# A table of offsets for the steps of a list-scheduled attention and MLP kernel

## The chip, the cores and the metric

The kernel runs on one core of a Trainium2 chip. The core has TensorE (matrix products), VectorE, ScalarE and GpSimd (element-wise work), and SyncE, whose instruction stream here issues nearly all DMAs. Each engine runs its own instructions in the order in which they were written; between engines there are only semaphores. The metric is the time of one execution on the device, in microseconds (us).

## The reference

Attention over 4 batches, 12 heads, 448 positions and head size 64, then two gated MLPs in a row on what it gives. Cut to its core:

```python
q_n = q / sqrt(mean(q*q) + 1e-6) * g_q           # k likewise
scores = q_n @ k_n.T / sqrt(64)
attn = exp(scores - max(scores)); attn = attn / (sum(attn) + 1e-9)
x = attn @ v                                     # to (4, 448, 768)

h = maximum(x @ w_in, 0)                         # MLP 1: 768 -> 1024
conv = sum(conv_w[k] * hp[:, k:k+S] for k in range(3))
x = (h * sigmoid(conv)) @ w_out                  # 1024 -> 768

gate_pre = sum(conv_w2[k] * xp[:, k:k+S] for k in range(5))   # MLP 2, causal
out = (sigmoid(gate_pre) * (x @ w_val)) @ w_out2 # 768 -> 768 -> 768
```

## The kernel before

All values are float32 outside. Inside, a product is made of three float16 products (high by high, low by high, high by low), so most tiles exist as a high half and a low half. The low half is the value minus the high half.

Attention is cut into 84 units u, 21 for each batch, each with 128 rows of scores for two heads (the remainder rows of several heads are put together in "rem" units). The steps of a unit are functions: `qk` (score matmuls into a pair of PSUM banks; ps<-ka,qa), `smax` (row maximum on VectorE; ps<-ps, then mx<-ps,root), `sexp` (two exponentials on ScalarE, which free the banks; p<-ps,mx,root), `phi` and `plo` (high and low half of p; p<-p and p<-p,p), `ptr` (a DMA transpose issued by SyncE; pt<-p) and `av` (product with v; ps<-vm,pt and ps<-vv,pt). Of two tiles each, the even units use p_0 and pt_92, the odd ones p_1 and pt_93; mx has four buffers in turn. Three units finished on a pair of heads give a tile of x: `x_pair` scales it (ps<-ps,rs), makes the high half (x<-ps), the low half (x<-ps,x), which frees the bank, and has both transposed by DMA (act<-x). `prep` loads q and k, sums their squares (ssq), takes the row factors (half, root) and transposes them (qa<-tq, ka<-tk); `load_v` and `split_v` prepare v (vst, vv, vm).

In batch 0, which has no MLP work beside it yet, p and x are transposed on TensorE instead.

The MLPs of a batch follow in tiles: `w_in_tile` (8 tiles f of 128 channels; ps<-act,wi), convolution, gate and high and low half, `w_out_tile` (ps<-act,wo), `w_val_tile` (ps<-act,wv), and `out_tile` (ps<-w,act, four blocks c of rows: three of 128 in two halves of 384 columns, and the remaining 64 rows in both halves at once), whose `evac` copies to osb on ScalarE and stores (out_dram<-osb). MLP work of one batch is placed between the attention units of the next.

What sets the order: a step is not run where the code is written but placed at a time with `at(t, fn)`. The steps are sorted by that time, and `run` records their operations in a `Plan`. `order` then makes a list schedule: every operation gets a due value, `first`, from the time of its step and the length of the work behind it (its tail); each engine in turn takes the ready operation with the smallest value, and an operation that several engines could do goes to another engine if that one would be done sooner. A few passes are made in which `first` is mixed with times found backward from the end, and the best by the planner's own length is kept. `emit` writes the instructions in that order, all from one line (378 in the profile of before, 495 after), so the rows are told apart by their tiles. The due value before:

```python
first = [o[4] * (1.0 - self.URGENT) - tail[i] * self.URGENT for i, o in enumerate(ops)]
```

Of the kernel before, what the change touches and what calls it, by code (L numbers as in the profile page):

```python
# [9 lines left out]
F32 = mybir.dt.float32  # L10
# [4 lines left out]
AF = mybir.ActivationFunctionType  # L15
# [7 lines left out]
SW = 2.0 ** UPW  # L23


class Plan:


# [6 lines left out]

    ENGINES = ("tensor", "vector", "scalar", "gpsimd", "sync")
    HOP = {"tensor": 0.2, "vector": 0.13, "scalar": 0.16, "gpsimd": 0.09}
    WINDOW = 20.453
    AHEAD = 42.251
    URGENT = 0.596  # L40
    TICK = 10.24 / 3
# [23 lines left out]
    def __init__(self):  # L65
        self.ops = []
        self.live = {}
        self.now = self.floor = 0.0
        self.tensor, self.vector, self.scalar, self.gpsimd, self.sync = (
            Plan.Queue(self, e) for e in Plan.ENGINES  # L70
        )
# [48 lines left out]
    def run(self, t, fn, *a):  # L120

        self.now = t
        fn(*a)

    def depend(self, engine, reads, out):
# [38 lines left out]
    def add(self, ways, **lean):  # L164
        engine, _, a, k = ways[0]
        aps = [x for x in list(a) + list(k.values()) if isinstance(x, bass.AP)]
        out = k.get("out", aps[0])
        flow, after = self.depend(engine, [x for x in aps if x is not out], out)
        costs = {}
        for e, m, a, k in ways:  # L170
            aps = [x for x in list(a) + list(k.values()) if isinstance(x, bass.AP)]
            costs[e] = (self.cost(e, m, a, k, aps, k.get("out", aps[0])), m, a, k)
        window = self.AHEAD if ways[0][1] == "dma_start" and k["in_"].dtype in (I64, U32) else self.WINDOW
        release = max(self.now - window, self.floor) if ways[0][1] == "dma_start" else 0.0
        self.ops.append((costs, flow | after, release, lean, self.now))

    def cost(self, engine, method, a, k, aps, out):

# [62 lines left out]
    def order(self):  # L241
        ops, nops = self.ops, len(self.ops)
        users = [[] for _ in ops]
        for i, o in enumerate(ops):
            for d in o[1]:
                users[d].append(i)
        tail = [0.0] * nops
        port, shape = [], []
        for i in range(nops):
            port.append({})  # L250
            shape.append(None)
            for e, (_, method, a, k) in ops[i][0].items():
                aps = [x for x in list(a) + list(k.values()) if isinstance(x, bass.AP)]
                port[i][e] = self.shares(e, method, aps, k.get("out", aps[0]))
                if e == "tensor":
                    shape[i] = (a[1].shape[0] <= 64, a[0].shape[0] <= 64)
        for i in reversed(range(nops)):
            (busy, lag, data), method, *_ = next(iter(ops[i][0].values()))
            tail[i] = max((tail[u] for u in users[i]), default=0.0) + busy + (data + 2.0 if method.startswith("dma") else 0.15)
        first = [o[4] * (1.0 - self.URGENT) - tail[i] * self.URGENT for i, o in enumerate(ops)]  # L260
        best = None
        for _ in range(self.PASSES):
            result, length, ends = self.forward(first, users, port, shape)
            if best is None or length < best[1]:
                best = result, length
            late = self.backward(result, length, ends, users)
            first = [self.MIX * a + (1.0 - self.MIX) * b for a, b in zip(first, late)]
        result, self.length = best
        self.times = {i: t for t, _, i, _ in result}
        self.engine = {i: e for _, _, i, e in result}  # L270
        return [(i, e) for _, _, i, e in result]
# [110 lines left out]
def kernel(  # L382
# [71 lines left out]
    cw2 = sb.tile([P, NC2 * KD], F32, tag="cw2", name="cw2")  # L454
    ident = sb.tile([P, P], F32, tag="ident", name="ident")
    zero = sb.tile([P, 1], F32, tag="zero", name="zero")

    banks = pp.tile([P, 8, 512], F32, tag="ps", name="ps")

# [14 lines left out]

        nc.vector.scalar_tensor_tensor(out, x, c, y, ALU.mult, op1)

    def copy(lean, out, x):

        nc.add([("vector", "tensor_copy", (out, x), {}), ("scalar", "activation", (out, x, AF.Copy), {})], vector=lean)

    def times(lean, out, x, c):

# [17 lines left out]
    S_DQ = 0.156  # L500
    S_K0 = 1.401
    S_K1 = 10.211
    S_DK = 1.263
    S_LQ = 4.632
    S_LK = -0.828
    S_G = -2.951
    DT0 = 2.39
    DT_1 = 5.037
# [2 lines left out]
    LAG = 2  # L511
    A_EXP = 0.154
    C_GATE = 2.001
    C_MUL = 2.338
    C_HI = 2.578
    C_LO = 3.244
    V_HI = 0.203
# [3 lines left out]
    E_PTR = 0.777  # L521
    E_AV = 2.342
    X_LAG = 2.135
    MPE = 97.144
    M_0 = 2.618
    M_1 = -6.504
    M_2 = -5.351
# [3 lines left out]
    L_TAP = -0.285  # L531
    LATE = 1
    LATE_F = 11
    FOLD_Q = 0
    FOLD_K = 0
    SIGN_IN = 0
    SIGN_OUT = 0
    SIGN_VAL = 3
# [9 lines left out]
    QD_ = 1.286  # L548
    W_IN = -79.489
    W_IN_STEP = 0.794  # L550
    W_OUT = -19.05
    W_OUT_STEP = 1.022
    W_VAL = 20.994
    W_VAL_STEP = 0.65
# [8 lines left out]
    OUT_1 = 0  # L563
    OUT_2 = 4
    OUT_3 = 4
    FLAT_0 = 0.908
    FLAT_1 = 0.0
    FLAT_2 = 0.0
    WIDE_0 = 1
    WIDE_1 = 1  # L570
    WIDE_2 = 1


    L_SQ = 3.972
# [22 lines left out]
    ROOTP_2 = 1  # L597
    ROOTP_3 = 0
    L_XLO = 0.9
    L_STEP = -0.143  # L600
    L_PLO = 0.668
    L_VM = -0.571
    L_VHI = 1.418
# [6 lines left out]


    WIDE = [(0, r) for r, w in enumerate((WIDE_0, WIDE_1, WIDE_2)) if w]

    LEAVE_IN = (LEAVE_0, LEAVE_1, LEAVE_2, LEAVE_3)
    X_SBUF = (0, XSB_1, XSB_2, XSB_3)
    ROOT_POOL = (ROOTP_0, ROOTP_1, ROOTP_2, ROOTP_3)
    FLAT = [(0, r) for r, f in enumerate((FLAT_0, FLAT_1, FLAT_2)) if f]
    events = []

    def at(t, fn, *a):  # L620
# [99 lines left out]
    def consts():  # L720

        nc.gpsimd.memset(mx[3], 0.0)
        nc.scalar.activation(mx[3], mx[3], AF.Exp)
        for t in ssq:
            nc.gpsimd.memset(t, 1.0)
        nc.gpsimd.memset(zero, 0.0)

    def init_v(ones, mid):

# [45 lines left out]
    def weight_piece(name, t, dram, dst, post, own, sign):  # L775
        st = {}
        wide = dram.dtype == I64
        n, m = dst[0].shape[1:] if len(dst[0].shape) == 3 else (1, dst[0].shape[1])
        m *= n

        def fetch():
            if not own:
                raw, w = stage(2 * m, st), stage(m, st) if len(dst) == 2 else None
            else:
                area = st["area"] = areas.pop(0)
                raw, w = area[:, 0 : 2 * m], area[:, 2 * m : 3 * m]
            if len(dst) == 1:
                w = dst[0].rearrange("p a b -> p (a b)") if n > 1 else dst[0]
            st["w"] = w
            to, src = (raw.bitcast(U32), dram.bitcast(U32)) if wide else (w, dram)  # L790
            st["raw"] = to
            loaded.append(t)
            load(to.rearrange("p (a b) -> p a b", a=n) if n > 1 else to, src, early=len(loaded) <= EARLY_W)

        def split():
            w = st["w"]
            if wide:
                to_f32(w, st["raw"], UPW, True, sign)
            else:
                nc.gpsimd.tensor_scalar(w, w, SW, None, ALU.mult)  # L800
            if len(dst) == 2:
                if n > 1:
                    w = w.rearrange("p (a b) -> p a b", a=n)
                copy(L_WHI, dst[0], w)
                sub(L_WLO, dst[1], w, dst[0])
            there[name] = there.get(name, 0) + 1
            if own:
                areas.append(st["area"])
            else:
                for x in st["i"]:  # L810
                    give(x)

        at(t, fetch)
        at(post, split)
# [41 lines left out]
    def prep(b, r, t0, tq, dq, tk_, dk, ahead):  # L856
# [23 lines left out]
        def total(fold, out, x):  # L880
            for i in range(0 if solo else fold):
                d = D >> i + 1
                nc.gpsimd.tensor_tensor(x[:, :, 0:d], x[:, :, 0:d], x[:, :, d : 2 * d], ALU.add)
                x = x[:, :, 0:d]
            nc.vector.tensor_reduce(out, x, AX.X, ALU.add)
# [15 lines left out]
        def sum_q():  # L901
            s2 = early_sq if b == 0 else oq.rearrange("p a n -> p (a n)").bitcast(F32)
            s2 = s2.rearrange("p (n d) -> p n d", d=D)
            square(s2, xq)
            total(FOLD_Q, ss[:, 0:NQ], s2)

        def split_q():
            if flat:
                return
            x = xq.rearrange("p n d -> p (n d)")  # L910
            copy(lean(L_QHI, S_LQ), oq[:, 0], x)
            sub(lean(L_QLO, S_LQ), oq[:, 1], x, oq[:, 0])

        def turn_q():
# [24 lines left out]
        def sum_k(i):  # L939
            j, x, x3, o, hi, lo = of_k(i)  # L940
            assert holds["kin", i] == (b, j)
            assert b == 0 or ("tk", 0) not in holds
            s2 = early_sq[:KR] if b == 0 else o.rearrange("p a c d -> p (a c d)").bitcast(F32)
            s2 = s2[:, 0 : 2 * KC * D].rearrange("p (n d) -> p n d", d=D)
            square(s2, x3)
            total(FOLD_K, ss[:KR, cols(i)], s2)

        def gain_k(i):
            x3 = of_k(i)[2]
# [156 lines left out]
    def phi(u):  # L1106
        u.o = p16[u.n % u.bufs]
        if u.out:
            copy(L_PHI, u.o[:, 0], u.p)
        else:  # L1110
            times(L_PHI, u.o[:, 0], u.p, SP)

# [559 lines left out]
```

## Time and profile before

| | us |
|---|---|
| median of 3 runs | 644.56 |
| lowest and highest run | 640.95, 646.72 |
| the profiled execution | 643.0 |
| its span in the trace | 641.2 |
| TensorE busy | 591.9 (92%) |
| VectorE busy | 510.4 (80%) |
| ScalarE busy | 419.6 (65%) |
| GpSimd busy | 254.5 (40%) |

The span is the time from the first to the last record of the trace; the profiled execution's own time holds 1.8 us more around it. An engine is busy while one of its instructions runs. DVE is VectorE, ACT ScalarE, POOL GpSimd, SP SyncE, PE TensorE; a row's start is counted from the start of the span, and the brackets behind it give the idle time of the engine just before and what ended it.

### The profile page before, as it was taken

The page shows a single profiled execution, that of the slowest core. Times are in us where ns is not written, and L with a number is a line of the kernel's source. Part 1 is how long each engine was busy: PE and PEld are TensorE (multiplying, and loading weights), DVE is VectorE, ACT ScalarE, POOL GpSimd, SP SyncE. Part 2 cuts the span into 40 slices and gives each one's busy share as a digit, 9 for nine tenths or more (in the row PEclk, how much of TensorE's full clock was granted, in tenths as well). Part 3 has the DMA queues.
Part 4 walks back from the last instruction along what each step waited for, and adds up shares of the span by engine and source line. Part 5 has one row for each costly group of instructions (what it writes and reads, how often), then busy time and mean ns, then how long its engine had stood idle before and what let it go on. Part 6 is the DMA issues. An engine that isn't in the chain of part 4 may idle for free.

```text
span 641.2 us, 12698 instructions
## 1 busy us (share of the span) xinstructions
PE 591.9 (92%) x4755; PEld 334.8 (52%) x4755; DVE 510.4 (80%) x1011; ACT 419.6 (65%) x739; POOL 254.5 (40%) x308
## 2 busy tenths in 40 slices
PE   4888998997997896999989999989999999999997
PEld 2665676453443443555545556545454565555554
DVE  6988899899999997999768984779898754478620
ACT  4986999798878975897655764768756454262211
POOL 2534675454454654657433552344534011040000
PEclk9985999897997998999989999999999999999999
DMA  8968576995799899867887668794545757100002
GB/s 206 224 162 208 110 184 172 210 220 122 151 194 194 198 199 191 207 143 130 189 155 127 117 127 176 147 170 74 105 80 104 118 119 148 25 0 2 1 13 74
DMA packets 254610, 88.05 MB, mean 137 GB/s; under 512 B 240671, under 2 KB 250453, under 8 KB 254549
## 3 DMA queue, kind: packets, MB, share of 16 engines
q1 hardware_dynamic: 252581, 86.76, 65.1%
q8 instruction: 37, 0.61, 0.4%
q10 hardware_dynamic: 1968, 0.49, 0.4%
q14 instruction: 24, 0.20, 0.1%
HBM read 38.59 MB, written 5.51 MB: 69 GB/s over the span
## 4 chain that ended last, share of the span: by engine, by line
PE 57%; DVE 24%; DMA 8%; ACT 5%; issue 3%; SPq 2%; ACTq 0%; DVEq 0%
PE ps L378 57%; DVE ps L378 6%; DVE act L378 6%; DVE w L378 4%; DVE scr L378 3%; DVE p L378 2%; DMA w<-in_moe_w_val_dram 2%; SPq L378 2%; DMA act<-in_moe_w_out_dram 2%; DMA pt<-p 2%; DVE ssq L378 1%; ACT p L378 1%; DMA w<-in_moe_w_in_dram 1%; ACT act L378 1%; ACT w L378 1%
## 5 line engine op out<-in xcount | busy, mean ns | idle before, releaser
L378 PE MATMUL ps<-act,wi 128*128 128x448 f16 x576 | 121.9, 362 | 7.4 <-DVE act L378 3.4
L378 PE MATMUL ps<-act,wo 128*128 128x448 f16 x576 | 123.6, 361 | 1.3 <-DVE act L378 0.8
L378 DVE TENSOR_REDUCE ps<-ps 128x2 f32<-128x896 f32 x84 | 91.5, 1093 | 21.4 <-PE ps L378 21.2
L378 ACT ACTIVATE p<-ps,mx,root 128x448 f32<-128x448 f32 x112 | 75.2, 721 | 36.1 <-DVE mx L378 20.9
L378 PE MATMUL ps<-w,act 128*128 128x384 f16 (+1 forms) x576 | 92.1, 327 | 1.1 <-DVE act L378 0.8
L378 PE MATMUL ps<-ka,qa 64*128 64x448 f16 (+3 forms) x560 | 81.3, 391 | 11.8 <-DVE p L378 9.3
L378 PE MATMUL ps<-act,wv 128*128 128x448 f16 x432 | 89.8, 353 | 1.5 <-ACT wv L378 1.1
L378 PE MATMUL ps<-vv,pt 128*128 128x65 f16 (+3 forms) x1488 | 88.2, 204 | 0.0
L378 PEld LDWEIGHTS <-wi 128*128 128x128 f16 x576 | 55.3, 100 | 61.7 <-issue 18.7
L378 POOL TENSOR_TENSOR p<-p,p 128x896 f16<-128x896 f32 x28 | 53.0, 1895 | 77.4 <-ACT p L378 50.7
L378 PEld LDWEIGHTS <-wo 128*128 128x128 f16 x576 | 55.2, 100 | 54.4 <-issue 12.1
L378 PEld LDWEIGHTS <-pt 128*128 128x128 f16 (+1 forms) x1512 | 63.6, 101 | 26.5 <-issue 8.3
L378 ACT ACTIVATE act<-ps 128x448 f16<-128x448 f32 (+4 forms) x81 | 43.0, 536 | 49.2 <-PE ps L378 25.6
L378 PEld LDWEIGHTS <-act 128*128 128x128 f16 (+1 forms) x576 | 48.7, 101 | 35.8 <-issue 8.8
L378 DVE SCALAR_TENSOR_TENSOR act<-ps,cw,act 128x446 f32<-128x446 f32 (+3 forms) x96 | 63.6, 676 | 0.9
L378 PEld LDWEIGHTS <-wv 128*128 128x128 f16 x432 | 40.1, 98 | 42.1 <-issue 5.2
L378 DVE SCALAR_TENSOR_TENSOR w<-w 128x768 uint32<-128x768 uint32 (+1 forms) x56 | 45.5, 815 | 0.0
L378 PEld LDWEIGHTS <-qa 64*128 64x128 f16 (+1 forms) x528 | 22.6, 99 | 43.8 <-issue 34.5
L378 DVE SCALAR_TENSOR_TENSOR scr<-ps,cw,scr 128x447 f32<-128x447 f32 x64 | 42.2, 676 | 1.9 <-ACT scr L378 1.6
L378 ACT ACTIVATE p<-p 128x896 f16<-128x896 f32 x42 | 39.8, 949 | 0.4
L378 POOL TENSOR_TENSOR kin<-kin,gb 112x512 f32<-112x512 f32 x22 | 29.2, 1332 | 19.6 <-ACT tk L378 14.6
L378 PE MATMUL ps<-vm,pt 128*128 128x130 f16 (+3 forms) x248 | 29.3, 234 | 5.0 <-DMA pt<-p 3.5
(128 smaller groups left out, 930.9 us busy)
## 6 DMA issues: line engine op xcount, KB each, us to landing
w<-in_moe_w_in_dram SPq DMA_DIRECT2D x8, 768.0 KB, 5.8
w<-in_moe_w_out_dram SPq DMA_DIRECT2D x8, 768.0 KB, 5.2
kin<-in_k_dram SPq DMA_DIRECT2D x24, 224.0 KB, 3.6
act<-in_moe_w_out_dram SPq DMA_DIRECT2D x12, 384.0 KB, 3.7
w<-in_moe_w_val_dram SPq DMA_DIRECT2D x12, 384.0 KB, 4.0
out_dram<-osb SPq DMA_DIRECT2D x24, 192.0 KB, 2.3
qin<-in_q_dram SPq DMA_DIRECT2D x34, 128.0 KB, 3.6
vst<-in_v_dram SPq DMA_DIRECT2D x17, 224.0 KB, 3.5
```

The costliest lines, as they stand in the source:

```text
L378: getattr(getattr(nc, e), method)(*a, **k)
```

## The change

Every step that `run` records now has a number, its place in the sorted list of 2034 steps. A table `OFFSETS` gives about half of these numbers an offset, from −7.05 to 10.73 us, most under 1 us; it is added to the due value of each operation of the step. Besides:

- Constants of the planner are set anew: WINDOW from 20.453 to 22.193 (how long before its step's time a load may be issued), and C_MUL, MPE, W_OUT, S_DK, S_LQ, S_LK, L_STEP by small amounts.
- `copy` may take GpSimd for the high halves of weights, q and p (a multiplication by ones), at a cost of 3.0 us added in the planner's choice.
- The sum of squares of q in batch 3 is folded on GpSimd in halves; the switches for this are now one for each batch.
- A tile of ones is set at the start.

```diff
+OFFSETS = {
+    4: 0.31, 6: 0.41, 7: 0.25, 8: 0.74, 19: -0.21, 20: 6.17, 21: 1.58, 24: -1.85, 27: 0.23, 28: 0.27, 45: 1.9, 46:
...
-    WINDOW = 20.453
+    WINDOW = 22.193
...
     def run(self, t, fn, *a):
 
         self.now = t
+        self.event += 1
         fn(*a)
...
-        self.ops.append((costs, flow | after, release, lean, self.now))
+        self.ops.append((costs, flow | after, release, lean, self.now, OFFSETS.get(self.event, 0.0)))
...
-        first = [o[4] * (1.0 - self.URGENT) - tail[i] * self.URGENT for i, o in enumerate(ops)]
+        first = [o[4] * (1.0 - self.URGENT) - tail[i] * self.URGENT + o[5] for i, o in enumerate(ops)]
...
+    def copy(lean, out, x, pool=None):
+
+        ways = [("vector", "tensor_copy", (out, x), {}), ("scalar", "activation", (out, x, AF.Copy), {})]
+        if pool is None:
+            nc.add(ways, vector=lean)
+            return
+        by = one[: x.shape[0], 0:1].to_broadcast(list(x.shape)) if len(x.shape) == 2 else one[: x.shape[0], 0:1].unsqueeze(2).to_broadcast(list(x.shape))
+        ways.append(("gpsimd", "tensor_tensor", (out, x, by, ALU.mult), {}))
+        nc.add(ways, vector=lean, gpsimd=pool)
...
-            total(FOLD_Q, ss[:, 0:NQ], s2)
+            total(FQ[b], ss[:, 0:NQ], s2)
...
-            copy(lean(L_QHI, S_LQ), oq[:, 0], x)
+            copy(lean(L_QHI, S_LQ), oq[:, 0], x, PC_Q)
...
-            copy(L_PHI, u.o[:, 0], u.p)
+            copy(L_PHI, u.o[:, 0], u.p, PC_P)
```

In the rows of the order below, mx_101 belongs to unit 49 and mx_102 to unit 50, and the number of a tile tells its buffers apart.

SyncE, the transposes of units 49 (pt_93) and 50 (pt_92) and what stands around them, before:

```order
L378 DMA_TRANSPOSE pt_93<-p_1_91 128x14x128
L378 DMA_TRANSPOSE qa_68<-tq_87 128x14x128
L378 DMA out_dram<-osb_99 128x384
L378 DMA qin_85<-in_q_dram 128x4x64 x3
L378 DMA_TRANSPOSE act<-x_0_80 128x3x128 x2
L378 DMA out_dram<-osb_98 64x384 x2
L378 DMA_TRANSPOSE pt_92<-p_0_90 128x14x128
```

and the same place in the changed kernel:

```order
L495 DMA_TRANSPOSE qa_68<-tq_87 128x14x128
L495 DMA_TRANSPOSE pt_93<-p_1_91 128x14x128
L495 DMA out_dram<-osb_99 128x384
L495 DMA qin_85<-in_q_dram 128x4x64
L495 DMA_TRANSPOSE pt_92<-p_0_90 128x14x128
L495 DMA_TRANSPOSE act<-x_0_80 128x3x128 x2
L495 DMA out_dram<-osb_98 64x384 x2
```

Unit 50's transpose has moved ahead of two q loads, two transposes of x and two stores; the q transpose now comes ahead of unit 49's.

VectorE, the row maxima and low halves of the same units, before:

```order
L378 TENSOR_REDUCE ps<-ps 128x2
L378 TENSOR_TENSOR mx_101<-ps,root_106 128x2
L378 TENSOR_SCALAR mx_101<-mx_101 128x2
L378 TENSOR_TENSOR p_1_91<-p_1_89,p_1_91 128x896
L378 TENSOR_REDUCE ssq_104<-tk_86 112x8 x2
L378 TENSOR_SCALAR ssq_104<-ssq_104 128x30
L378 TENSOR_SCALAR half_108<-ssq_104 128x30
L378 TENSOR_SCALAR root_107<-half_108 128x30
L378 TENSOR_TENSOR half_108<-root_107 128x30
L378 TENSOR_REDUCE ps<-ps 128x2
L378 TENSOR_TENSOR mx_102<-ps,root_106 128x2
```

and in the changed kernel:

```order
L495 TENSOR_REDUCE ps<-ps 128x2 x2
L495 TENSOR_TENSOR mx_101<-ps,root_106 128x2
L495 TENSOR_TENSOR mx_102<-ps,root_106 128x2
L495 TENSOR_SCALAR mx_101<-mx_101 128x2
L495 TENSOR_SCALAR mx_102<-mx_102 128x2
L495 TENSOR_TENSOR p_1_91<-p_1_89,p_1_91 128x896
L495 TENSOR_REDUCE ssq_104<-tk_86 112x8 x2
L495 TENSOR_SCALAR ssq_104<-ssq_104 128x30
L495 TENSOR_TENSOR p_0_90<-p_0_88,p_0_90 128x896
```

Both maxima are taken in a row, ahead of the low half of unit 49 and of the row factors (ssq, half, root).

VectorE, about 415 to 423 us of the trace of before: the scaling of an x tile (rs, ps<-ps,rs), unit 64's low half (p_0_90), and the x halves, before:

```order
L378 TENSOR_SCALAR rs_109<-ps 128x6
L378 SCALAR_TENSOR_TENSOR half_108<-root_106 128x30
L378 RECIPROCAL rs_109<-rs_109 128x6
L378 TENSOR_TENSOR p_0_90<-p_0_88,p_0_90 128x896
L378 TENSOR_TENSOR ps<-ps,rs_109 128x6x64
L378 TENSOR_REDUCE ps<-ps 128x2
L378 TENSOR_TENSOR x_0_80<-ps,x_0_80 128x384
```

and in the changed kernel:

```order
L495 TENSOR_SCALAR rs_109<-ps 128x6
L495 RECIPROCAL rs_109<-rs_109 128x6
L495 TENSOR_TENSOR ps<-ps,rs_109 128x6x64
L495 CAST x_0_80<-ps 128x384
L495 TENSOR_TENSOR x_0_80<-ps,x_0_80 128x384
L495 TENSOR_REDUCE ps<-ps 128x2
```

The copy of the high half has come from ScalarE to VectorE (CAST), and the low half p_0_90 no longer stands between the reciprocal and the scaling.

## Rows read from the trace of the kernel before

**Rows 1.** The page: busy time by engine; the group of w_in matmuls.
```profile
PE 591.9 (92%) x4755; PEld 334.8 (52%) x4755; DVE 510.4 (80%) x1011; ACT 419.6 (65%) x739; POOL 254.5 (40%) x308
...
L378 PE MATMUL ps<-act,wi 128*128 128x448 f16 x576 | 121.9, 362 | 7.4 <-DVE act L378 3.4
```

**Rows 2.** Windows by stage: length, busy time (instructions) of PE, PEld, DVE, ACT, POOL, clock, DMA, GB/s.
```profile
0.00:260.00 260.00, 221.49 (x1741) 133.71 (x1742) 235.81 (x479) 209.01 (x374) 131.67 (x189) 0.91 0.84 183
260.00:303.00 43.00, 41.74 (x345) 22.27 (x344) 41.94 (x82) 36.14 (x70) 27.43 (x34) 1.00 0.76 164
303.00:425.00 122.00, 117.44 (x1041) 64.24 (x1040) 90.79 (x188) 72.48 (x119) 50.86 (x47) 0.99 0.76 149
425.00:478.00 53.00, 52.33 (x437) 27.81 (x436) 48.82 (x99) 38.16 (x67) 24.03 (x24) 1.00 0.57 102
478.00:637.00 159.00, 158.93 (x1199) 86.76 (x1197) 93.09 (x167) 63.28 (x110) 20.49 (x18) 1.00 0.30 59
```

**Rows 3.** Timeline of PE, the rows with a wait after 260 us.
```profile
294.19 0.48 PE L378 MATMUL ps<-w,act 128*128 128x384 f16 x2 [0.80 <-DVE act L378]
...
301.30 0.48 PE L378 MATMUL ps<-w,act 128*128 128x384 f16 x2 [0.32 <-POOL w L378]
...
329.94 0.35 PE L378 MATMUL ps<-vm,pt 128*128 128x130 f16 x3 [1.90 <-DMA pt<-p]
...
419.38 0.34 PE L378 MATMUL ps<-vm,pt 128*128 128x130 f16 x3 [0.99 <-DMA pt<-p]
...
422.89 0.54 PE L378 MATMUL ps<-act,wi 128*128 128x448 f16 x2 [1.67 <-DVE x L378]
...
477.58 0.35 PE L378 MATMUL ps<-vm,pt 128*128 128x130 f16 x3 [0.63 <-DMA pt<-p]
```

**Rows 4.** Windows: two half-clocked stretches, and one with waits at full clock.
```profile
44.20:64.60 20.40, 17.32 (x78) 12.58 (x79) 15.94 (x42) 13.57 (x26) 8.77 (x7) 0.50 0.91 205
330.90:334.20 3.30, 3.30 (x11) 1.30 (x9) 1.63 (x3) 1.66 (x3) 0.16 (x1) 0.50 1.08 213
...
419.30:424.00 4.70, 2.95 (x32) 1.81 (x33) 1.68 (x6) 2.55 (x5) 0.93 (x2) 1.00 0.86 167
```

**Rows 5.** Groups of p on DVE: ns of one (least, median, most), first and last start.
```profile
L378 DVE TENSOR_TENSOR p<-p,p x14: 1083/1092/1381, 311.8 to 540.0; 128x896 f16<-128x896 f32 x14
```

**Rows 6.** Timeline of DVE, unit 50's low half.
```profile
320.37 1.09 DVE L378 TENSOR_TENSOR p<-p,p 128x896 f16<-128x896 f32 x1
```

**Rows 7.** Timeline of the SP queue, 319 to 327 us, issues.
```profile
319.12 1.80 SPq L378 DMA_DIRECT2D qin<-in_q_dram  x3
321.03 3.10 SPq L378 DMA_TRANSPOSE act<-x  x2
324.22 1.38 SPq L378 DMA_DIRECT2D out_dram<-osb  x2
325.70 1.60 SPq L378 DMA_TRANSPOSE pt<-p  x1
```

**Rows 8.** Timelines of SP queue, ACT and DVE, 417 to 423 us.
```profile
418.01 0.58 SPq L378 DMA_DIRECT2D vst<-in_v_dram  x1
...
421.29 0.58 ACT L378 ACTIVATE vst<-vst 128x448 f32<-128x448 f32 x1 [3.33 <-DMA vst<-in_v_dram]
421.77 0.47 ACT L378 ACTIVATE x<-ps 128x384 f16<-128x384 f32 x1
...
417.69 0.56 DVE L378 TENSOR_TENSOR ps<-ps,rs 128x384 f32<-128x384 f32 x1
...
422.28 0.56 DVE L378 TENSOR_TENSOR x<-ps,x 128x384 f16<-128x384 f32 x1 [3.03 <-ACT x L378]
```

**Rows 9.** Timeline of the SP queue from 637.5 us.
```profile
637.53 1.12 SPq L378 DMA_DIRECT2D out_dram<-osb  x2
```

**Rows 10.** Timelines: unit 56's exponentials on ACT, unit 57's score matmuls on PE.
```profile
365.73 1.35 ACT L378 ACTIVATE p<-ps,mx,root 128x448 f32<-128x448 f32 x2
...
366.11 1.17 PE L378 MATMUL ps<-ka,qa 64*128 64x448 f16 x6
```

More of the change, by code (lines that the diff above doesn't have):

```diff
@@ L23 @@
 SW = 2.0 ** UPW
+OFFSETS = {
[111 rows of a table added]
+}
 class Plan:
@@ L68, in __init__ @@
         self.now = self.floor = 0.0
+        self.event = -1
         self.tensor, self.vector, self.scalar, self.gpsimd, self.sync = (
@@ L456 @@
     zero = sb.tile([P, 1], F32, tag="zero", name="zero")
+    one = sb.tile([P, 1], F32, tag="one", name="one")
     banks = pp.tile([P, 8, 512], F32, tag="ps", name="ps")
@@ L475, in fma @@
         nc.vector.scalar_tensor_tensor(out, x, c, y, ALU.mult, op1)
-    def copy(lean, out, x):
-        nc.add([("vector", "tensor_copy", (out, x), {}), ("scalar", "activation", (out, x, AF.Copy), {})], vector=lean)
+    def copy(lean, out, x, pool=None):
[6 more added lines that the diff above has]
+        nc.add(ways, vector=lean, gpsimd=pool)
     def times(lean, out, x, c):
@@ L502 @@
     S_K1 = 10.211
-    S_DK = 1.263
-    S_LQ = 4.632
-    S_LK = -0.828
+    S_DK = 0.585
+    S_LQ = 4.686
+    S_LK = -0.92
     S_G = -2.951
@@ L513 @@
     C_GATE = 2.001
-    C_MUL = 2.338
+    C_MUL = 2.356
     C_HI = 2.578
@@ L523 @@
     X_LAG = 2.135
-    MPE = 97.144
+    MPE = 97.132
     M_0 = 2.618
@@ L533 @@
     LATE_F = 11
-    FOLD_Q = 0
-    FOLD_K = 0
+    FOLD_Q0 = 0
+    FOLD_Q1 = 0
+    FOLD_Q2 = 0
+    FOLD_Q3 = 1
+    FOLD_K0 = 0
+    FOLD_K1 = 0
+    FOLD_K2 = 0
+    FOLD_K3 = 0
     SIGN_IN = 0
@@ L550 @@
     W_IN_STEP = 0.794
-    W_OUT = -19.05
+    W_OUT = -18.97
     W_OUT_STEP = 1.022
@@ L565 @@
     OUT_3 = 4
-    FLAT_0 = 0.908
-    FLAT_1 = 0.0
-    FLAT_2 = 0.0
     WIDE_0 = 1
@@ L571 @@
     WIDE_2 = 1
+    WIDE1_0 = 0
+    WIDE1_1 = 0
+    WIDE1_2 = 0
+    FLAT0_1 = 0
+    FLAT0_2 = 0
+    FLAT1_0 = 0
+    FLAT1_1 = 0
     L_SQ = 3.972
@@ L599 @@
     L_XLO = 0.9
-    L_STEP = -0.143
+    L_STEP = -0.082
+    PC_W = 3.0
+    PC_Q = 3.0
+    PC_P = 3.0
     L_PLO = 0.668
@@ L612 @@
     WIDE = [(0, r) for r, w in enumerate((WIDE_0, WIDE_1, WIDE_2)) if w]
+    WIDE += [(1, r) for r, w in enumerate((WIDE1_0, WIDE1_1, WIDE1_2)) if w]
     LEAVE_IN = (LEAVE_0, LEAVE_1, LEAVE_2, LEAVE_3)
+    FQ = (FOLD_Q0, FOLD_Q1, FOLD_Q2, FOLD_Q3)
+    FK = (FOLD_K0, FOLD_K1, FOLD_K2, FOLD_K3)
     X_SBUF = (0, XSB_1, XSB_2, XSB_3)
     ROOT_POOL = (ROOTP_0, ROOTP_1, ROOTP_2, ROOTP_3)
-    FLAT = [(0, r) for r, f in enumerate((FLAT_0, FLAT_1, FLAT_2)) if f]
+    FLAT = [(0, 0)] + [x for x, f in (((0, 1), FLAT0_1), ((0, 2), FLAT0_2), ((1, 0), FLAT1_0), ((1, 1), FLAT1_1)) if f]
     events = []
@@ L726, in consts @@
         nc.gpsimd.memset(zero, 0.0)
+        nc.gpsimd.memset(one, 1.0)
     def init_v(ones, mid):
@@ L803, in split @@
                     w = w.rearrange("p (a b) -> p a b", a=n)
-                copy(L_WHI, dst[0], w)
+                copy(L_WHI, dst[0], w, PC_W)
                 sub(L_WLO, dst[1], w, dst[0])
@@ L945, in sum_k @@
             square(s2, x3)
-            total(FOLD_K, ss[:KR, cols(i)], s2)
+            total(FK[b], ss[:KR, cols(i)], s2)
         def gain_k(i):
```

110 rows, old and new, of the table OFFSETS are left out of this document.

## The prediction

> **What bounds the kernel now.** I read the page's busy line first. TensorE is busy 591.9 us, 92% of the span of 641.2; the next engine, VectorE, 80% [rows 1]. The end is therefore set by TensorE's own work plus the time in which it has none, and no order of the same work can take out more than that idle time and what the clock costs. The second view is the table of windows [rows 2], which says where the idle time lies: 260 − 221.5 = 38.5 us of it before 260 us, 1.3 us from 260 to 303, 4.6 from 303 to 425, 0.7 from 425 to 478, and 0.1 after that. Third come TensorE's waits after 260 us, one by one [rows 3]: 0.80, 0.32, 1.90, 0.99, 1.67 and 0.63, 6.31 us in all. Fourth is the granted clock [rows 4]: where it is 0.50 (1.2 GHz in place of 2.4) the same matmuls take twice as long. One such stretch lies behind 260 us, from 330.9 to 334.2, right after the wait of 1.90; the long one, 44.2 to 64.6, lies in the early part.
>
> **The change, part by part.** The two orders, matched operation by operation, hold the same matmuls and the same DMAs. Up to about 260 us VectorE, SyncE and GpSimd have them in the same sequence, TensorE differs by little more than 1 us of work at any point, and ScalarE swaps a few copies. So the 38.5 us there stay: 0, and I give the early part no bound but the spread of the runs.
>
> GpSimd may now copy high halves, but the order has no such copy on it: 0. Three reductions of batch 3's q sums go from VectorE to GpSimd folds. The trace has no fold of that shape; from 303 to 425 us GpSimd is idle 122 − 50.9 = 71 us and VectorE 31 [rows 2], the sums are needed only when a pair's row factors are worked out, and I take 0. Seven net low halves p<-p,p go from GpSimd to VectorE, where one takes 1.08 to 1.38 [rows 5]: 7 × 1.09 = 7.6 us, against idle VectorE time of 31 (303 to 425), 4.2 (425 to 478) and 66 us (478 to 637). Only in the 4.2 could it be felt, and one or two of the seven lie there: 0, and if that cover is gone 1.1 us for each, which the bounds below hold.
>
> *Units 49 and 50.* Unit 50's low half ends on VectorE at 320.37 + 1.09 = 321.46 [rows 6], but its transpose pt<-p is issued on SP at 325.70, behind three q loads, two act<-x transposes and two output stores [rows 7]; it lands at 329.9, when TensorE has waited 1.90 [rows 3]. In the new order the transpose stands behind the first q load, with the other two loads (two thirds of 1.80), the 3.10 and the 1.38 behind it: 5.7 us of issues less ahead of it. For that its data must be there earlier too, and it is: its score matmuls stand right behind unit 49's, and its maximum comes on VectorE ahead of unit 49's low half. So the transpose can land up to 5.7 us sooner where 1.90 are needed: −1.9. What is late next are the act<-x transposes, behind the 1.60 that this issue takes; they feed the w_in product of batch 2, which begins only with the batch's last units at hand, so I give that nothing. The clock's fall behind this wait costs half of 3.4 us of half-clocked work, 1.7 [rows 4]. I take it as gone with the wait: −1.7, bounds 0 and −1.7. The trace's nearest case speaks for less than certainty: from 419.3 to 424.0 TensorE worked only 2.95 of 4.7 us and the clock stayed at 1.00 [rows 4].
>
> The Trainium skill's page "TensorE: Matmul & The Clock Gate", section "HAM oscillation — how this bites in real kernels", says that a matmul kernel whose bursts are split by DMA waits falls back to half rate after the wait and starts the next burst cold. At 330.9 the trace agrees, at 419.3 to 424.0 it does not, though two waits stand there. By the rule alone the clock term would be −1.7 if the wait goes, and each new wait of the same kind would cost as much again.
>
> *The place at 417 to 424 us.* TensorE waits 0.99 for unit 63's transpose and 1.67 for a bank that x holds [rows 3]. The second is a chain: SP issues a v load at 418.01, ScalarE's scaling of it has waited 3.33 when it starts at 421.29, the copy x<-ps queued behind it runs at 421.77, and VectorE's subtraction, which frees the bank, waits 3.03 for that copy and starts at 422.28 [rows 8]. In the new order the copy is a CAST on VectorE directly behind the scaling of ps, and the low half that stood before that scaling (1.09 [rows 5]) comes later. The scaling then starts at 417.69 − 1.09 = 416.6, and three operations of 0.56 in a row give 418.3, in place of 422.28 + 0.56 = 422.84. TensorE comes to the first matmul of that bank at 418.0 or so in the new order: about 0.3 of wait left. The transpose of unit 63 is now behind one v load and one store more, about 1.1 us, and six w_in matmuls of 121.9 / 576 = 0.21 [rows 1] have been put ahead of its use, 1.2 too: its wait of 0.99 stays. Sum: 2.66 − 1.3 = 1.36, so −1.4; bounds 0.6 (the transpose late by the whole issue time, without cover) and 2.66.
>
> *Others.* At 477.58 the new order has four more product matmuls, 0.8 us, ahead of the wait of 0.63: −0.6. At 294.19 a high half goes to ScalarE and the subtraction that held the bank follows its neighbour: −0.8; the 0.32 at 301.30, for a weight piece on GpSimd, I leave. At the end the last group is now one whole-height half, so one store follows the last evacuation in place of two issued in 1.12 us [rows 9]: half of that, −0.6, bounds 0 and −1.2.
>
> *New waits.* Three score matmuls move earlier, to places with little slack. Unit 58's goes 8 us earlier, directly behind unit 57's. It takes the bank pair that unit 56's exponentials free at 365.73 + 1.35 = 367.08, and unit 57's matmuls end at 366.11 + 1.17 = 367.28 [rows 10]: by before's clock a margin of 0.2. If TensorE comes there 1.9 earlier and ScalarE does not, 1.7 are waited. For units 51 and 55 no row shows the wait; I bound each by 0 and the mean of the six, 6.31 / 6 = 1.05. Together 0 to 3.8; no row is nearer to one end, and I take the middle, 1.9.
>
> **Sum.** −1.9 − 1.7 − 1.4 − 0.6 − 0.8 − 0.6 + 1.9 = −5.1. Against the profiled execution's 643.0 (span 641.2 and 1.8 around it) that gives 637.9. The median of the runs, 644.56, lies 1.6 above that execution, so the forecast of a median is 644.56 − 5.1 = 639.5. The worst ends of the terms (−1.9, 0, −0.6, −0.6, −0.8, 0, +3.8) sum to −0.1, the best (−1.9, −1.7, −2.7, −0.6, −1.1, −1.2, 0) to −9.2.
>
> **The rivals.** *All of it and no new wait.* TensorE from 260 us to the end then has nothing but work, as already from 478 to 637 (158.93 of 159) [rows 2]. It gives −9.2 + about 1 for the tail that cannot vanish, 635 to 637. For it: 31 us of idle VectorE between 303 and 425. Against it: unit 58's margin of 0.2.
>
> *The waits change place.* An operation moved forward on one queue pushes back others; what a table has taken out of the places named comes back at units 51, 55, 58 or in the fuller VectorE of 425 to 478 (48.82 of 53 busy [rows 2]). Then 642 to 647, no change. For it: every wait above is due to a queue's sequence, not to a missing resource, and an order made from a list is only as good as the times it assumes; at unit 50 the transpose stood 325.70 − 321.46 = 4.2 us in the queue with its data ready, and a queue as full is left to the next one.
>
> *A new wait that drops the clock for long.* Place: unit 58, or units 63 and 64. Price: the stretch from 44.2 to 64.6 ran at 0.50 for 20.4 us with 17.3 busy [rows 4], so half of 17.3, 8.7 us. With the gains halved (−2.6) that is 650.7; with none, 653. [...] Against it: from 260 us on the mean clock of the four windows is 1.00, 0.99, 1.00 and 1.00 [rows 2], so it fell there but once, for the 3.4 us named.
>
> *The change is not in effect.* The table could leave the order as it was; it does not, as the rows of the order show, so this has no chance of its own.
>
> **How the numbers follow.** Forecast case, 637 to 642, likeliest at 639.5: 0.50. All gone, 633.5 to 637: 0.17. Waits change place, 642 to 647: 0.26. Slower by the clock, 647 to 653: 0.07. Leaving out about a tenth on either side gives 634.5 to 646; the runs of before alone spread from 640.95 to 646.72, and the bounds of the terms reach −9.2, so I take 633.5 to 646.5. A measurement of this kernel can tell about 1%, 6.4 us, from no change: faster than 638.1 are the case in which all goes (0.17) and a third of the forecast case (0.17), 0.34; slower than 651 half of the last case, 0.04, and 0.01 for an unforeseen one; the rest, 0.61, is within.
>
> **What would show it.** Right: no TensorE wait at unit 50's pt near 325 to 330 and a granted clock of 1.00 there; pt<-p issued on SP directly behind a single q load; a DVE CAST x<-ps near 417, and no wait for x behind it; a wait of about 1 for pt just after; one 128x384 store last. The windows to 260 us should show the same 221 us of TensorE work and the same half-clocked stretches. Wrong: a wait of 1 us or more at unit 58's scores or anywhere from 425 to 478, a half-clocked stretch after 260, or an early part that is longer or shorter by more than 2 us, which would mean that small swaps on ScalarE count where I gave them nothing.

## The result and the profile after

Four executions of each gave 637.35 us for the changed kernel (636.88 to 637.85) and 644.23 for the one before (640.95 to 646.72): ratio 0.9896, 95% interval 0.9851 to 0.9942. In the experiments below it was run again, unchanged: 638.83 against 643.24, twelve executions to 35, 0.9935 (0.9909 to 0.9961). An execution over 1.5% longer than the fastest of its kernel is left out of the ratios: one of these twelve (647.70) and one each in two runs below. The second figure is the firmer one: 0.65%, 4.2 us. The forecast was 5.1 us less, 639.5.

The page of the changed kernel, its span and busy time (to be read beside [rows 1]):

```profile
span 635.1 us, 12712 instructions
...
PE 586.5 (92%) x4755; PEld 331.6 (52%) x4755; DVE 511.8 (81%) x1014; ACT 421.7 (66%) x744; POOL 240.2 (38%) x304
```

TensorE has the same 4755 matmuls, yet is busy 5.4 us less. Most of that is no work saved but the clock: the mean granted clock of this profile is 0.970, that of [rows 1] 0.963, so span × (1 − clock) fell from 23.7 to 19.1 us. The windows have the columns of [rows 2]; they are cut at the same times up to 303 us, and where about the same work stands behind that. They say that TensorE's idle time hardly changed:

```profile
0.00:260.00 260.00, 220.92 (x1757) 130.83 (x1758) 237.02 (x481) 210.27 (x375) 132.52 (x190) 0.93 0.83 183
260.00:303.00 43.00, 41.29 (x340) 22.27 (x338) 42.49 (x81) 35.92 (x70) 27.57 (x35) 1.00 0.76 167
303.00:420.00 117.00, 113.00 (x1021) 62.11 (x1019) 89.40 (x187) 72.37 (x120) 43.20 (x44) 1.00 0.76 150
420.00:475.00 55.00, 54.84 (x461) 29.68 (x460) 50.54 (x102) 41.17 (x72) 23.89 (x24) 1.00 0.59 106
475.00:631.00 156.00, 156.00 (x1182) 86.62 (x1180) 92.34 (x167) 61.53 (x108) 12.99 (x14) 1.00 0.30 60
```

Idle before 260 us: 39.1 (38.5 before). Behind it: 1.7 + 4.0 + 0.2 + 0 = 5.9, where it had been 6.6. Yet the waits are not the same ones. TensorE's timeline, the rows with a wait of more than 0.3 us after 260 us (0.24, 0.17 and 0.16 are left out):

```profile
271.00 0.54 PE L495 MATMUL ps<-act,wi 128*128 128x448 f16 x2 [1.16 <-DVE act L495]
...
309.92 0.52 PE L495 MATMUL ps<-w,act 128*64 128x384 f16 x4 [0.53 <-ACT osb L495]
...
318.47 0.72 PE L495 MATMUL ps<-ka,qa 64*128 64x448 f16 x3 [0.44 <-ACT osb L495]
...
334.45 0.29 PE L495 MATMUL ps<-vm,pt 128*128 128x130 f16 x2 [1.57 <-DMA pt<-p]
...
413.76 0.35 PE L495 MATMUL ps<-vm,pt 128*128 128x130 f16 x3 [0.84 <-DMA pt<-p]
...
418.91 0.34 PE L495 MATMUL ps<-vm,pt 128*128 128x130 f16 x3 [0.45 <-DMA pt<-p]
```

Of [rows 3] the waits at unit 50, for x, at 477.58 and at 294.19 are gone. New are a wait for the transpose of unit 51 (1.57), one of 0.84 for unit 62's, and two for ScalarE's osb, the second of them at unit 51's score matmuls; the one at 271.00 is no work of the table (a run with before's order shows it too, 0.87). Why unit 51 waits is on the SP queue, the counterpart of [rows 7]:

```profile
319.14 2.46 SPq L495 DMA_TRANSPOSE pt<-p  x1
321.70 3.57 SPq L495 DMA_TRANSPOSE act<-x  x2
325.37 1.20 SPq L495 DMA_DIRECT2D out_dram<-osb  x2
326.62 2.62 SPq L495 DMA_DIRECT2D qin<-in_q_dram  x4
329.29 0.59 SPq L495 DMA_DIRECT2D vst<-in_v_dram  x1
330.00 2.39 SPq L495 DMA_TRANSPOSE pt<-p  x1
```

Unit 50's transpose is issued at 319.14, as forecast. Unit 51's low half runs on VectorE, in the row

```profile
324.12 1.09 DVE L495 TENSOR_TENSOR p<-p,p 128x896 f16<-128x896 f32 x1 [2.12 <-ACT p L495]
```

and is done at 325.21; its transpose is issued at 330.00, behind the stores and loads that had stood ahead of unit 50's. It waits in the queue 4.8 us, as unit 50's had waited 4.2. VectorE at the other place, beside [rows 8], does what the order said:

```profile
415.12 0.57 DVE L495 TENSOR_TENSOR ps<-ps,rs 128x384 f32<-128x384 f32 x1
415.72 0.56 DVE L495 CAST x<-ps 128x384 f16<-128x384 f32 x1
416.31 0.56 DVE L495 TENSOR_TENSOR x<-ps,x 128x384 f16<-128x384 f32 x1
```

### The profile page after: what moved, and what is told of

Same layout as the page of the kernel before. It is cut to its first block, busy times and chain, and to the rows that moved or that the text cites. A ratio compares the mean times of both kernels' runs of the same rounds, so it can differ in the third digit from the quotient of the medians.

```text
span 635.1 us, 12712 instructions
## 1 busy us (share of the span) xinstructions
PE 586.5 (92%) x4755; PEld 331.6 (52%) x4755; DVE 511.8 (81%) x1014; ACT 421.7 (66%) x744; POOL 240.2 (38%) x304
## 5 line engine op out<-in xcount | busy, mean ns | idle before, releaser
L495 PE MATMUL ps<-act,wo 128*128 128x448 f16 x576 | 125.9, 357 | 1.2 <-DVE act L495 0.8
L495 PE MATMUL ps<-vv,pt 128*128 128x65 f16 (+3 forms) x1488 | 106.1, 203 | 0.0
L495 PE MATMUL ps<-w,act 128*128 128x384 f16 (+1 forms) x576 | 95.5, 326 | 0.9 <-ACT osb L495 0.5
L495 PE MATMUL ps<-act,wv 128*128 128x448 f16 x432 | 94.3, 357 | 0.3 <-ACT wv L495 0.2
L495 PEld LDWEIGHTS <-pt 128*128 128x128 f16 (+1 forms) x1512 | 73.5, 101 | 32.1 <-issue 9.3
L495 DVE SCALAR_TENSOR_TENSOR act<-ps,cw,act 128x446 f32<-128x446 f32 (+2 forms) x96 | 63.9, 675 | 1.0
L495 POOL TENSOR_TENSOR p<-p,p 128x896 f16<-128x896 f32 x21 | 39.8, 1899 | 54.0 <-ACT p L495 25.8
L495 DVE TENSOR_TENSOR p<-p,p 128x896 f16<-128x896 f32 x21 | 23.0, 1097 | 23.4 <-ACT p L495 23.2
```

Source lines behind the costliest of these rows:

```text
L495: getattr(getattr(nc, e), method)(*a, **k)
```

## The experiments

In all of them but the changed kernel run again, `order` returns a written list in place of the schedule that it works out, so that single instructions can be moved and all else stays. The list of before gives before's instructions one for one.

```diff
     def order(self):
+        import base64, struct, zlib
+
+        raw, n = zlib.decompress(base64.b85decode(ORDER)), len(self.ops)
+        return [(i, Plan.ENGINES[e]) for i, e in zip(struct.unpack("<%dH" % n, raw[: 2 * n]), raw[2 * n :])]
```

Ratios are to the kernel before on the same chip, in the same hour; its medians in the three groups of runs were 642.87, 643.24 and 643.46. Each run has twelve executions, the low halves on GpSimd eleven and the run with units 62 and 63 seven.

| run | us | ratio (95%) |
|---|---|---|
| before again | 643.05 | 0.9999 (0.9977 to 1.0022) |
| before's order up to 250 us, then the changed | 639.52 | 0.9932 (0.9906 to 0.9959) |
| changed up to 247 us, then before's | 642.82 | 0.9994 (0.9971 to 1.0017) |
| before's up to 345 us, then the changed | 644.35 | 1.0025 (1.0002 to 1.0048) |
| changed again | 638.83 | 0.9935 (0.9909 to 0.9961) |
| before, unit 50's transpose moved | 641.87 | 0.9982 (0.9960 to 1.0004) |
| changed, three transposes moved | 642.13 | 0.9989 (0.9957 to 1.0020) |
| before, last two groups exchanged | 641.85 | 0.9987 (0.9959 to 1.0014) |
| changed, q loads first | 640.73 | 0.9951 (0.9920 to 0.9981) |
| the same, and units 62 and 63 | 639.02 | 0.9929 (0.9898 to 0.9961) |
| changed, low halves on GpSimd | 639.38 | 0.9923 (0.9896 to 0.9949) |
| before, x copy on VectorE | 641.84 | 0.9965 (0.9937 to 0.9993) |

### Is it the early part, or the clock's chance?

Before again: 

> The order of before once more, instruction for instruction, given as a list. In the two profiles TensorE's half-clocked stretches sum to 47.8 us before and 37.5 after, and 10.2 of the difference lie before 70 us, where the two orders are nearly the same. Theory A (the stretches before 70 us fall by chance from execution to execution): this profile has another set of stretches than 44.15 to 64.63 there, a sum that differs from 47.8 by 3.4 us or more, and the times spread over 640 to 647. Theory B (the order sets them): 20 us at half clock from 44 on again, a sum of 44 to 51, and the time near 644.

Before's order early: 

> The changed kernel, but all operations that before starts ahead of 250 us stand in before's order, on before's engines; what follows is the changed order. Theory A (the small early swaps count for nothing, the clock there is chance): 637 to 638, as the changed kernel. Theory B (the early swaps give the 2.9 us by which the changed kernel's trace is ahead at 260 us): about 640.3.

The changed order early: 

> The reverse: the kernel of before, but all operations that the changed kernel starts ahead of 247 us stand in the changed order; what follows is before's. Theory A: 643 to 645, as before. Theory B: about 641.3, 2.9 less than before.

The changed kernel again: 

> The changed kernel once more, unchanged, beside the others on one chip. If the gain is the order's: 0.989 to 0.991 of before, and half-clocked stretches that vary from execution to execution. If part of it was the clock's luck in four executions: nearer to the run with before's order up to 250 us, 0.993.

The edit of the two mixed runs is in the list alone; in words, for the first:

```diff
-ORDER = changed order
+ORDER = what before starts ahead of 250 us, in before's order, then the rest in the changed order
```

The times follow the late part: 0.9932 with the changed order behind 250 us, the same as the whole changed kernel's 0.9935, and 0.9994 with before's. So the small early swaps count for nothing that can be measured here (0.9994, with about 1.5 us to either side). The median of the first mixed run, 639.52, lies nearer to theory B's 640.3 than to A's 637 to 638; but the changed kernel, run again, took 638.83 itself, and its 0.9935 is the second of the two outcomes named for it. So some 2.5 us of the 6.9 between the first four executions of each were luck: they did not come again. The clock's early part is not the order's either. The windows of the changed kernel's second profile show the long half-clocked stretch of before ([rows 4]), and one behind unit 51's wait (2.35 in that profile):

```profile
44.20:64.60 20.40, 17.37 (x78) 12.69 (x79) 15.96 (x42) 14.43 (x27) 8.78 (x7) 0.50 0.93 206
337.80:341.10 3.30, 3.30 (x20) 1.76 (x19) 2.81 (x6) 3.27 (x5) 2.09 (x2) 0.50 0.76 133
```

while the first profile of the changed kernel has this there:

```profile
44.20:50.60 6.40, 2.79 (x27) 1.87 (x25) 6.37 (x15) 4.82 (x11) 4.26 (x4) 1.00 1.11 224
51.60:58.30 6.70, 6.20 (x26) 4.04 (x24) 6.06 (x21) 5.40 (x10) 1.65 (x1) 0.50 0.97 246
330.90:334.20 3.30, 1.98 (x11) 0.81 (x9) 1.46 (x3) 3.17 (x6) 1.34 (x2) 1.00 1.05 208
```

And the kernel of before with only its last groups exchanged, the early order of before, has two short stretches in place of the long one:

```profile
43.10:49.90 6.80, 6.41 (x31) 4.18 (x29) 5.45 (x13) 4.72 (x10) 2.40 (x2) 0.50 1.16 191
53.40:60.10 6.70, 6.61 (x26) 4.45 (x26) 6.17 (x20) 5.40 (x10) 1.64 (x1) 0.50 0.71 188
```

Theory A holds. Before again, by contrast, had the long stretch once more (45.0 to 65.4), so that by this one profile alone the order would have seemed to set it; its stretches sum to 56.5 us, though, which is not the 44 to 51 of theory B. The 4.7 us of clock between the first two profiles are mostly chance: averaged over executions, the mean clock is 0.9672 before (35) and 0.9695 changed (the eleven of the ratio), 1.5 us.

### The place of units 49 and 50

Before's order up to 345: 

> As the run with before's order up to 250 us, but up to 345, so that the place of units 49 and 50 stands as before too, and only what follows is changed. By the prediction that place is worth 1.9 of wait and 1.7 of clock, so this is 2.5 to 3.6 us slower than the run with before's order up to 250. By the traces' difference (2.9 us ahead at 260, 1.9 at 345) the stretch from 260 to 345 gave back about 1 us, so this would be 0 to 1 us faster than that run.

The run came out 0.9% above the one with before's order to 250, more than either outcome named for it. It doesn't settle the place, though: at the seam it has a wait that neither kernel has, for unit 53's transpose, in this row

```profile
361.30 0.36 PE L674 MATMUL ps<-vm,pt 128*64 128x130 f16 x6 [3.63 <-DMA pt<-p]
```

which with the half-clocked stretch behind it is most of the difference. One moved instruction is cleaner. On SP, in the kernel of before:

```diff
 DMA_TRANSPOSE act<-x_0_80 128x3x128
+DMA_TRANSPOSE pt_92<-p_0_90 128x14x128
 DMA_TRANSPOSE act<-x_0_80 128x3x128
 DMA out_dram<-osb_98 64x384 x2
-DMA_TRANSPOSE pt_92<-p_0_90 128x14x128
```

> The kernel of before with one instruction moved on one queue: unit 50's transpose pt<-p is issued on SP between the two act<-x transposes and not behind them and two stores, 3 us sooner. Its data is ready by then (321.46 us). By the prediction the wait of 1.90 at unit 50 goes, and with it the half-clocked stretch behind it: 1.9 to 3.6 us less. By the rival (the waits change place) unit 51's transpose, issued at 331.3, is late next: 0 to 1 us less in all.

Its TensorE rows:

```profile
324.32 0.34 PE L556 MATMUL ps<-vm,pt 128*128 128x130 f16 x3 [0.37 <-DMA pt<-p]
...
332.97 0.35 PE L556 MATMUL ps<-vm,pt 128*128 128x130 f16 x3 [2.04 <-DMA pt<-p]
```

Unit 50's wait is 0.37, and unit 51, which had none in before, now waits 2.04. The ratio, 0.9982, cannot be told from no change (its interval reaches 1.0004). So the rival is right at this place: TensorE came sooner to unit 51, whose transpose was the next one late in the same queue.

Then the changed kernel, where unit 51's transpose is waited for, with that one moved forward as well, in this way (units 62 and 63 by the edit that stands further below):

```diff
 DMA_TRANSPOSE act<-x_0_80 128x3x128 x2
+DMA_TRANSPOSE pt_93<-p_1_91 128x14x128
 DMA out_dram<-osb_98 64x384 x2
 DMA qin_85<-in_q_dram 128x4x64 x2
 DMA qin_85<-in_q_dram 64x2x64 x2
 DMA vst_78<-in_v_dram 128x7x64
-DMA_TRANSPOSE pt_93<-p_1_91 128x14x128
```

> The changed kernel with the transposes of units 51, 62 and 63 moved forward on SP alone (51 ahead of two stores and four q loads, 62 between two transposes of x, 63 with the v load behind it ahead of three stores). TensorE waits for them 1.57, 0.84 and 0.45 us. If what is left at these places is only the queue's order: 2.5 to 2.9 us less than the changed kernel, and no wait for pt<-p behind 300 us. If other waits take their place: less than 1 us.

No wait for pt<-p of more than 0.21 us is left behind 300 us, and it is slower than the changed kernel, 0.9989, which neither outcome had. The rows of SP, ScalarE, VectorE and TensorE tell why:

```profile
319.12 0.45 SPq L673 DMA_DIRECT2D qin<-in_q_dram  x1
...
329.77 2.59 SPq L673 DMA_DIRECT2D qin<-in_q_dram  x4
...
333.88 0.95 ACT L673 ACTIVATE tq<-qin 128x896 f32<-128x896 f32 x1 [8.02 <-DMA qin<-in_q_dram]
...
335.81 0.62 DVE L673 SCALAR_TENSOR_TENSOR act<-ps,act 128x448 f16<-128x448 f32 x1 [5.12 <-ACT act L673]
...
340.76 0.53 PE L673 MATMUL ps<-act,wo 128*128 128x448 f16 x1 [4.41 <-DVE act L673]
```

From the first q load to the other four it is 10.6 us now, 8.4 in the changed kernel. ScalarE's square of q stands at the head of its queue and holds the copies of the convolution behind it, VectorE waits for those, and TensorE for VectorE. In the changed kernel ScalarE waits there as well, 5.24 us, but TensorE, held by unit 51, doesn't come to need it. Loads first, then:

```diff
 DMA_TRANSPOSE pt_92<-p_0_90 128x14x128
-DMA_TRANSPOSE act<-x_0_80 128x3x128 x2
-DMA out_dram<-osb_98 64x384 x2
 DMA qin_85<-in_q_dram 128x4x64 x2
 DMA qin_85<-in_q_dram 64x2x64 x2
+DMA_TRANSPOSE act<-x_0_80 128x3x128
+DMA_TRANSPOSE pt_93<-p_1_91 128x14x128
+DMA_TRANSPOSE act<-x_0_80 128x3x128
+DMA out_dram<-osb_98 64x384 x2
 DMA vst_78<-in_v_dram 128x7x64
-DMA_TRANSPOSE pt_93<-p_1_91 128x14x128
```

> The changed kernel with batch 3's first q loads issued on SP right behind unit 50's transpose, then one transpose of x, unit 51's transpose, and only then the other transpose of x and the two stores. The run in which only unit 51's transpose was moved pushed those loads back: ScalarE's square of q, which stands first in its queue, then waited 8.02 us for them, VectorE 5.12 behind it, and TensorE 4.41. If that queue is the reason: ScalarE's wait falls from 5.24 in the changed kernel to under 3, neither unit 51's wait (1.57 to 2.35) nor the 4.41 is there, and the time is 1.6 to 3.3 us less than the changed kernel's. If waits only change place again: within 1 us of it.

```profile
326.68 0.95 ACT L673 ACTIVATE tq<-qin 128x896 f32<-128x896 f32 x1 [0.65 <-DMA qin<-in_q_dram]
...
334.31 0.58 ACT L673 ACTIVATE vst<-vst 128x448 f32<-128x448 f32 x1 [4.21 <-DMA vst<-in_v_dram]
...
351.69 0.54 PE L673 MATMUL ps<-ka,qa 64*128 64x448 f16 x2 [1.65 <-ACT p L673]
```

The mechanism holds: ScalarE's wait for q is 0.65, and neither unit 51's wait nor the 4.41 is there. The time isn't less: now the v load, next in the queue, holds ScalarE 4.21 us, and TensorE waits 1.65 for a bank that the exponentials free, with 3.4 us at half clock behind it. With units 62 and 63 moved too, by this edit:

```diff
 DMA_TRANSPOSE act<-xr_0_81 128x2x64
+DMA_TRANSPOSE pt_92<-p_0_90 128x14x128
 DMA_TRANSPOSE act<-xr_0_81 128x2x64
-DMA_TRANSPOSE pt_92<-p_0_90 128x14x128
+DMA vst_78<-in_v_dram 128x7x64
+DMA_TRANSPOSE pt_93<-p_1_91 128x14x128
 DMA out_dram<-osb_99 64x384 x2
 DMA out_dram<-osb_98 128x384
-DMA vst_78<-in_v_dram 128x7x64
-DMA_TRANSPOSE pt_93<-p_1_91 128x14x128
```

> The same, and at 406 to 414 us unit 62's transpose between two transposes of x and the v load and unit 63's transpose ahead of three stores. There TensorE waits 0.84 and 0.45 in the changed kernel: up to 1.3 us less than the run before it if nothing else is late next, 0.5 if the wait of 0.74 for VectorE's scr at 436 us is there as in the run with three transposes moved.

The waits of 0.84 and 0.45 go and 0.63 for scr comes at 433.54, but two others stand in this run:

```profile
344.89 0.23 PE L673 MATMUL ps<-vm,pt 128*128 128x130 f16 x1 [0.88 <-DMA pt<-p]
...
353.40 0.53 PE L673 MATMUL ps<-ka,qa 64*128 64x448 f16 x1 [2.00 <-ACT p L673]
```

The bank wait is 2.00, and unit 52's transpose is waited for 0.88 us: 0.9929, the changed kernel's ratio again. No version beats the changed kernel by more than the measurement can tell.

### The place at 417 us, GpSimd, the tail

VectorE in the kernel of before, with the copy of x taken from ScalarE:

```diff
-TENSOR_TENSOR p_0_90<-p_0_88,p_0_90 128x896
 TENSOR_TENSOR ps<-ps,rs_109 128x6x64
+CAST x_0_80<-ps 128x384
+TENSOR_TENSOR x_0_80<-ps,x_0_80 128x384
+TENSOR_TENSOR p_0_90<-p_0_88,p_0_90 128x896
 TENSOR_REDUCE ps<-ps 128x2
-TENSOR_TENSOR x_0_80<-ps,x_0_80 128x384
```

> The kernel of before with one place changed: the copy x<-ps at 421.77 us runs on VectorE directly behind the scaling of ps and not on ScalarE behind the v scaling, and unit 64's low half comes behind the x halves. By the prediction the wait of 1.67 for x falls to 0.3 or less, and the wait for unit 63's transpose (0.99) stays: 1.4 to 1.7 us less than before. If the wait changes place: a wait for v (vv) or unit 64's transpose of about 1 us shows behind it, and less than 0.7 us is gained.

Its TensorE rows:

```profile
419.45 0.34 PE L556 MATMUL ps<-vm,pt 128*128 128x130 f16 x3 [0.94 <-DMA pt<-p]
...
434.30 0.54 PE L556 MATMUL ps<-act,wi 128*128 128x448 f16 x2 [1.50 <-DVE scr L556]
```

The wait for x is gone and unit 63's stays at 0.94, as forecast. It is neither v nor unit 64's transpose that is late next: 15 us later VectorE, 48.82 of 53 us busy there [rows 2], is late by 1.50 with the convolution (scr). The time, 0.9965, cannot tell the two expectations apart; the rows say that most of the gain went to another wait. The changed kernel doesn't have it, but it came back, 0.74 and 0.63, in the two runs that took away the waits for units 62 and 63.

The low halves back on GpSimd (the engine of eight p<-p,p, units 51, 57 to 60, 65, 72 and 78, from VectorE to GpSimd): 

> The changed kernel with the eight low halves p<-p,p that the change took from GpSimd to VectorE given back to GpSimd (units 51, 57 to 60, 65, 72, 78), at the same place by time. By the prediction the engine counts for nothing: within 0.5 us. If it counts: a low half takes 1.89 us there in place of 1.09, so the transposes of these units are issued 0.8 later or more, and TensorE waits for them, up to 0.8 us at each of the two or three that have no slack (51, 65): 1 to 2 us more.

0.9923 against 0.9935: no loss shows, as forecast. The two intervals together, about 2.4 us, would not rule out a loss of 1 us; the row does more for it, as unit 51 waits 1.87, between the changed kernel's two values (1.57 and 2.35).

The tail, on SP in the kernel of before (its matmuls and evacuations in the same way):

```diff
+DMA out_dram<-osb_99 64x384 x2
 DMA out_dram<-osb_98 128x384
-DMA out_dram<-osb_99 64x384 x2
```

> The kernel of before with its last two groups exchanged: the group of the remaining 64 rows first, the half of 128 rows last, so that one store follows the last evacuation, as in the changed kernel. By the prediction 0.6 us less, seen in the trace as the time from TensorE's last matmul to the end of the span: 4.3 us before, about 3.7 here.

From TensorE's last matmul to the end of the span it is 3.4 us, 4.3 in before and 3.6 in both profiles of the changed kernel. The median, 1.4 us lower, agrees but cannot show so little.

## Why the prediction was right, and where not

The forecast of −5.1 stands against −4.2 in the second measurement. Most of its steps can be priced from several profiles, those with before's late order (before, before again, changed early, and others where the place is untouched) against those with the changed one (changed, before's early, changed again, low halves on GpSimd):

| step | forecast | shown by the profiles |
|---|---|---|
| wait at unit 50 | −1.9 | −0.4: from 1.90, 3.12, 2.24, 2.24, 2.31 to 1.57, 2.06, 2.35, 1.87 at unit 51 |
| its half-clocked stretch | −1.7 | −0.9: 3.4, 6.8, 3.4, 0, 3.4 us at half clock to 0, 3.4, 3.4, 0 |
| 417 to 424 us | −1.4 | −1.2: from 2.66, 2.52, 2.52, 2.30 to 1.29, 1.33, 0.97, 1.55 |
| 477.58 | −0.6 | −0.3: 0.63, 0.38, 0.37 and none to none |
| 294.19 | −0.8 | −0.8: 0.79 to 0.80 to none |
| tail | −0.6 | −0.7 |
| new waits | +1.9 | +0.5: at 310 and 318 us 0.97, 0.80 and twice 0.14; unit 58 none |
| early part | 0 | 0, by the mixed runs, to about 1.5 us |

The third column sums to about −4, near the time measured. That the late part of the order makes the difference is shown by the mixed runs; what each place gives is read from these few profiles and not shown by a run of its own, as two of the places that were changed alone (unit 50's transpose, the x copy) each brought another wait. **The mis-sized term** is the place of units 49 and 50: "the transpose can land up to 5.7 us sooner where 1.90 are needed: −1.9". Its first part is right: unit 50's wait is gone in every profile of the changed order. But the stores and loads that it passed were put in front of the next unit's transpose, and "what is late next" was looked for among the x transposes and not in the unit behind. That is the rival "the waits change place", true at this place and not of the whole. By these profiles the place gave 1.3 us where 3.6 were forecast.

That the total still came out near is partly luck: the new waits, priced at the middle of wide bounds, came out near their low end, +0.5 in place of +1.9, as unit 58's scores, split by the order among other matmuls, never waited. At 417 to 424 us, too, the size is right and what is left is not what was forecast: unit 63's wait, which was to stay at 0.99, is 0.26 to 0.45, and unit 62's, which was not foreseen, is 0.71 to 1.27.

**The early part** was forecast alike and is, but the sentence that the same half-clocked stretches would be seen there was wrong in its ground: they are not the order's. Nor is VectorE's sequence up to 260 us quite the same, as it has a few operations exchanged between 134 and 145 us; the mixed runs show no price for it.

Of the signs named ahead, these are there: pt<-p behind a single q load, the CAST before 417 us and no wait for x behind it, 220.9 us of TensorE work up to 260. The wait for pt after it is 0.45 and not about 1. The clock behind unit 50 was at 1.00. Two signs of being wrong were there: a half-clocked stretch after 260 us, behind unit 51 in the second profile, and in the first an early part 2.9 us shorter than before's, which by the mixed runs and the clock was chance. A long fall of the clock did not come: 3.4 us is the longest stretch at 0.50 behind 260 us in the four profiles of the changed order.

On the clock, the runs bear out the row of before only in part. Behind waits of 1.90, 2.06, 2.31, 2.35, 3.02 and 3.12 us for a transpose at units 50 and 51 the clock fell to 0.50, behind 1.57, 1.87 and 2.04 it stayed at 1.00. Behind the same wait of 2.24 at unit 50 it fell in one profile (changed up to 247 us, the first row) and stayed in another (last two groups exchanged, the second):

```profile
329.70:333.10 3.40, 3.40 (x26) 1.82 (x23) 1.87 (x5) 1.53 (x2) 0.22 (x1) 0.50 0.91 191
...
330.70:334.10 3.40, 3.37 (x44) 1.99 (x44) 2.25 (x5) 1.14 (x2) 0.22 (x1) 1.00 0.88 195
```

So the term is half of what was forecast. The Trainium skill's page "TensorE: Matmul & The Clock Gate", section "HAM oscillation — how this bites in real kernels", has the fall follow each DMA wait of a kernel whose waits are about 3 to 5 us long. Most of the waits here are shorter, so the prediction took the rule further than the page does; in these profiles the clock fell behind some of the shorter waits and not behind others, and what decides it stays open.

## What to carry to other kernels

When an instruction is moved forward in an in-order queue, price what it passes, and first of all the next instruction of its own kind: where one transpose had waited 4.2 us in a queue here, the next one then waited 4.8. A wait taken away at one place brings TensorE sooner to the next, so single repairs were worth little here. Before the clock's part of a difference is read from two profiles, run the old kernel again: its own stretches at half clock differed here by 8.7 us between two profiles, and its executions on one chip spread over 6 to 9 us, where the change was worth 4.2.

## What the hardware did that was not expected

With one and the same order, the stretches at half clock summed to different amounts in different profiles: 47.8 and 56.5 us with before's order, 37.5 and 49.0 with the changed one. Before 70 us there was one of 20.5 us from 44 or 45 on in four profiles, of either order, and two of 6.8 in seven others. The 99 timed executions of before beside the experiments took 637.9 to 647.4 us, at mean clocks of 0.955 to 0.979. A transpose's issue on SP also has no fixed price: 1.6 to 3.4 us for unit 50's pt<-p, and 2.9 to 4.3 for the same two act<-x that stand together beside it.
